# Regrouping rows six slots ahead of their premix, with eight buffers, in a fused attention and expert kernel

## The chip, the cores and the metric

The kernel runs on one core of one Trainium2 chip. The metric is the device time of one execution in microseconds (us). Three executions of the kernel before took 899.65, 904.73 and 894.24 us; their median is 899.65 us.

## The reference, cut to what matters

Three stages follow one another. The first is attention with "talking heads": the heads are mixed before and after the softmax. Here there are 4 batches, 12 heads, 448 positions, and 64 values per head.

```python
scores = scale * np.matmul(q, k.transpose(0, 1, 3, 2))
scores = np.einsum('bhij,hg->bgij', scores, w_pre)
attn = np.exp(scores - np.max(scores, axis=-1, keepdims=True))
attn = attn / (np.sum(attn, axis=-1, keepdims=True) + 1e-09)
attn = np.einsum('bhij,hg->bgij', attn, w_post)
out = np.matmul(attn, v)
```

Its output, as 1792 tokens of 768 values, goes through `h = x @ w_in; (h - tanh(h)) @ w_out` (stage 1) and then through a mixture of 8 experts with 4 slots each. The change lies in the attention and at its border to stage 1.

## The kernel before, in words

**Chunks and slots.** Each batch's 448 query rows are cut into chunks of 120, 120, 120 and 88 rows, 16 chunks in all. A chunk is worked in slots of at most 10 query rows: 12 slots for a chunk of 120, 10 for one of 88, so 184 slots. The chunks start at slots 0, 12, 24, 36, 46, 58, 70, 82, 92, 104, 116, 128, 138, 150, 162 and 174.

**What a chunk and a slot go through.** The scores of a chunk (L275, for two heads a call, six calls) are matmuls whose results ScalarE copies (L295) into a tile `S` with the query row on the partition. There are two `S` tiles, so the scores of chunk m go where those of chunk m-2 were. Head mixing wants the heads of a query row on the partition, so `regroup` (L308) moves the rows of one slot from `S` into a tile `D`, by one DMA on SyncE's queue (SP). There are `DB` of these tiles, used in turn. Two slots make a pair: at every even slot `premix` (L315) multiplies two `D` tiles by the mixing matrix and VectorE takes the maxima (L325); `expo` (L328) is ScalarE's exponential; `guard`, `recip` and `norm` (L337 to L351) make the second mixing matrix divided by the sums; `postmix` (L355) comes four slots later and `gather` (L369) copies its result; `values` (L392) multiplies by v.

**What sets the order.** Every engine works through its instructions in the order in which the program emits them. The main loop (L573) emits, at slot s: the regroup of slot s + `D_AHEAD` (L577), then the loads and stores planned for s (all on SP's queue), then, at an even s, premix, an earlier pair's postmix, expo and guard; at an odd s, recip, norm and gather; then two of the waiting copies of scores, then pieces of a conversion of the weights of stage 1 (loads at L88 and L94, six slots ahead of their use; stores at L120), then at most two waiting jobs (transposes of keys L235 and queries L258, and `values`).

A regroup waits, in SP's queue, for the premix that last read its `D` tile, and for the copies that filled its `S` tile. With `D_AHEAD` = 4 and `DB` = 6 the regroup of slot s + 4 goes to the tile of slot s - 2. The first copy of a chunk's scores into `S` waits until the last regroup of the chunk two before has landed.

**A planner** (L428 to L519) places the other work by slots. The three `head` groups of chunk m (scores of two pairs of heads each) start at the chunk before, at its start minus `D_AHEAD` plus 1 (L451 to L461), two slots after the chunk two before has had its last regroup issued. The keys of a batch are transposed beside them (L462 to L471), their loads at least six slots sooner. A chunk's queries are transposed in two halves in windows (L472 to L477), each in the slot with the least TensorE work planned; the loads of queries have windows of their own, which `D_AHEAD` does not enter. Conversion pieces are spread over the loop (L487). Loads with a window go where SP's plan is emptiest.

**The end.** At slot 184 - `D_AHEAD` (L614) the tiles of keys, queries, `S` and the conversion are given back, and stage 1's first weights and inputs are loaded into their space (L1168 to L1172). Stage 1's first work is emitted after the last slot (L1173).

Of the kernel before, what the change touches and what calls it, by code (L numbers as in the profile page):

```python
# [132 lines left out]
def talking_heads(tc, ident, q, k, v, w_pre, w_post, xd, box, follow):  # L133
# [2 lines left out]
    NC = len(chunks)  # L136
    slots = [(n, kk) for n in range(NC) for kk in range(len(chunks[n][3]))]
    NS = len(slots)
    D_AHEAD = 4
    DB = 6  # L140
    T_LAG = 4
    EB = T_LAG // 2 + 1
    WARM = 10
# [17 lines left out]
    def load_k(b, p):  # L161
        if b:
            t = er.tile([JP, NR, 2, HD], FP32, tag="kn", name="kn", bufs=NP)
            nc.sync.dma_start(out=t, in_=k[b, 2 * p:2 * p + 2].rearrange("e (p r) d -> p r e d", r=NR))
        else:
            t = er.tile([JP, 2, NR, HD], FP32, tag="kn", name="kn", bufs=NP)
            nc.sync.dma_start(out=t, in_=k[b, 2 * p:2 * p + 2].rearrange("e (p r) d -> p e r d", r=NR))
        nat_k[b, p] = t
# [8 lines left out]
    def load_q(n):  # L177
        b, i0, ni, _ = chunks[n]
        t = er.tile([CHUNK, NH, HD], FP32, tag="qn", name="qn")
        nc.sync.dma_start(out=t[:ni], in_=q[b, :, i0:i0 + ni, :].rearrange("h p d -> p h d"))  # L180
        nat_q[n] = t
# [121 lines left out]
    def rows(s):  # L303
        n, kk = slots[s]
        o, m = chunks[n][3][kk]
        return n, o, m

    def regroup(s):  # L308
        n, o, m = rows(s)
        t = ds[s % DB]  # L310
        ni, w = chunks[n][2], len(chunks[n][3])
        nc.sync.dma_start(out=t[4:4 + m * NH], in_=S_t[n][o:ni:w])
        D_t[s] = t
# [114 lines left out]
    start = [sum(len(c[3]) for c in chunks[:n]) for n in range(NC + 1)]  # L428
# [8 lines left out]
    def fetch(lo, hi, cost, f, *a):  # L437
        wanted.append((hi, lo, cost, f, a))

    def calm(kind, lo, hi):  # L440
        return min(range(lo, hi + 1), key=lambda s: (load[kind][s], s))

    def job(s, f, *a, act=0.0, dve=0.0, pe=0.0):
        plan("job", s, f, *a)
        load["pe"][s] += pe
        load["act"][s] += act
        load["dve"][s + 1] += dve

    for m in range(1, NC):
        w = len(chunks[m - 1][3])  # L450
        w0 = start[m - 1] - D_AHEAD  # L451
        for g in range(3):
# [9 lines left out]
    for m in range(1, NC):  # L462
        if chunks[m][1] + CHUNK >= SEQ and m + 1 < NC:
            w = len(chunks[m - 1][3])
            w0 = start[m - 1] - D_AHEAD
            free_at = {}
# [5 lines left out]
    for m in range(2, NC):  # L472
        t0 = start[m - 2]
        if m > 2:
            fetch(max(2, t0 - 12), t0 - 8 if t0 > 12 else max(2, t0 - 7), 0.7, load_q, m)
        for lo, hi, hf in ((max(2, t0 - D_AHEAD + 1), t0 + 3, 0), (t0 + 4, start[m - 1] - D_AHEAD - 1, 1)):
            job(calm("pe", lo, hi), q_half, m, hf, act=0.47, dve=0.53, pe=0.4)  # L477
    for m in range(NC):
        step = len(chunks[m + 1][3]) // 3 if m + 1 < NC - 1 else 2
        for g in range(3 if m + 1 < NC else 0):  # L480
            lo = start[m + 1] + T_LAG + 1 + g * step
# [4 lines left out]
    for i, j in enumerate(pieces):  # L486
        due = 6 + i * (NS - D_AHEAD - 17) // len(pieces)  # L487
        t0 = max(t, due)
# [36 lines left out]
    for p in (1, 2):  # L525
        load_k(0, p)
    ds = [lt.tile([128, SEQ], FP32, tag=f"D{i}", name="D", bufs=1) for i in range(DB)]
    et = [lt.tile([128, SEQ], FP32, tag=f"e{i}", name="e", bufs=1) for i in range(2 * EB)]
# [31 lines left out]
    load_q(2)  # L560
    for s in range(D_AHEAD):
        regroup(s)
# [10 lines left out]
    while s < NS:  # L573
        now[0] = s
        box["both"] = s < NS - D_AHEAD
        if s + D_AHEAD < NS:
# [862 lines left out]
def fused_kernel(  # L1439
# [57 lines left out]
    with tc.manual_schedule():  # L1497
        talking_heads(
            tc, ident, q, k, v, w_pre, w_post, xd, box,
            lambda: moe_and_slots(tc, ident, xd, wi, wo, wo4, wis, (tshift, tlimit, moe2_phi, sel, sela, seld), moe2_w1, moe2_w2, out, box))  # L1500
# [29 lines left out]
```

## Time and profile before

| | before |
|---|---|
| median of three executions | 899.65 us (894.24 to 904.73) |
| profiled execution | 899.93 us |
| span from first to last instruction | 898.2 us |
| mean granted TensorE clock | 0.978 |
| TensorE (PE) busy | 823.1 us, 92% |
| ScalarE (ACT) busy | 573.5 us, 64% |
| VectorE (DVE) busy | 556.1 us, 62% |
| SP's DMA queue, share of 16 engines | 74.4% over the span |

The attention takes the first 444 us or so of the span. All rows are of the one profiled execution, whose own time is 1.7 us above its span. In a row of the timeline a bracket says how long the engine sat idle before it and what ended that wait; the letters q after an engine's name mean its sequencer, which issues DMAs. Where several DMAs share a semaphore the name of the DMA in a bracket can be that of another DMA on the same semaphore.

### The profile page before, as it was taken

Reading aid. Unit: us, or ns where it says so; the run is one execution under the profiler, and the core shown is the slowest. Engines: PE = TensorE matmul, PEld = TensorE weight load, DVE = VectorE, ACT = ScalarE, POOL = GpSimd, SP = SyncE. Lnnn points to the kernel's source line nnn. Section 1 sums busy time; section 2 is a strip of 40 time slices with the busy share of each in tenths; the row PEclk is TensorE's granted clock in tenths of the full one; section 3 lists DMA queues with packets and bytes.
Section 4 is the critical chain, followed back from the end, with each engine's and each line's share of the span. In section 5 each row is a group of like instructions: output and inputs, shape, how many; then the busy total and the mean of one; then the engine's idle time right before and its main releaser. Section 6 shows DMA issues by size and latency. Waiting matters only on the chain.

```text
span 898.2 us, 28617 instructions
## 1 busy us (share of the span) xinstructions
PE 823.1 (92%) x11760; PEld 581.5 (65%) x11760; DVE 556.1 (62%) x1181; ACT 573.5 (64%) x1351; POOL 257.0 (29%) x438
## 2 busy tenths in 40 slices
PE   8878989889987999999999899999999989999995
PEld 6456666666655666666776676767767767864542
DVE  4456857677766777777467886557776767720103
ACT  4766877778867788878656775647555656621013
POOL 6343434444434334434212561000000035500000
PEclk9989999999999999999999999999999999997998
DMA  6988889887989888774869976688745445899997
GB/s 133 227 215 231 220 215 235 238 226 215 226 217 236 233 208 243 238 216 154 261 216 374 346 243 215 258 306 325 284 162 176 158 141 193 284 380 426 416 372 267
DMA packets 145622, 222.95 MB, mean 248 GB/s; under 512 B 60820, under 2 KB 127444, under 8 KB 142036
## 3 DMA queue, kind: packets, MB, share of 16 engines
q1 hardware_dynamic: 142144, 208.26, 74.4%
q10 hardware_dynamic: 3348, 12.87, 3.6%
q8 instruction: 93, 1.52, 0.7%
q14 instruction: 37, 0.30, 0.1%
HBM read 146.39 MB, written 36.18 MB: 203 GB/s over the span
## 4 chain that ended last, share of the span: by engine, by line
PE 57%; ACT 13%; DMA 12%; DVE 12%; issue 4%; POOL 1%; SPq 0%; ACTq 0%; POOLq 0%; DVEq 0%
PE hp L830 21%; DMA D<-S 9%; PE pm L321 5%; ACT e L333 5%; PE vx L403 5%; PE sc L287 4%; PE tm L364 4%; DVE mx L325 3%; PE h L1314 3%; ACT S L295 2%; PE so L1355 2%; PE gt L900 2%; PE tz L1334 2%; ACT aT L378 2%; PE lgp L984 2%
## 5 line engine op out<-in xcount | busy, mean ns | idle before, releaser
L333 ACT ACTIVATE e<-pm,mx 128x448 f32<-128x448 f32 x184 | 115.1, 632 | 81.8 <-DVE mx L325 78.5
L830 PE MATMUL hp<-xa,rg 128*128 128x512 f32 x576 | 153.1, 405 | 0.6 <-ACT xa L813 0.4
L325 DVE TENSOR_REDUCE mx<-pm 128x1 f32<-128x448 f32 x184 | 106.1, 618 | 76.2 <-PE pm L321 76.0
L364 PEld LDWEIGHTS tm<-wk,e 64*56 64x56 f32 x5888 | 108.5, 130 | 57.0 <-issue 30.7
L321 PE MATMUL pm<-D,wpre 64*64 64x448 f32 (+2 forms) x736 | 113.0, 566 | 19.1 <-DMA D<-S 16.8
L364 PE MATMUL tm<-wk,e 64*56 64x60 f32 x5888 | 117.5, 218 | 10.1 <-issue 5.3
L830 PEld LDWEIGHTS hp<-xa,rg 128*128 128x128 f32 x576 | 102.2, 188 | 30.0 <-issue 10.5
L295 ACT ACTIVATE S<-sc 120x448 f32<-120x448 f32 (+1 forms) x186 | 91.4, 552 | 13.8 <-DMA kn<-in_k_dram 5.8
L287 PE MATMUL sc<-khi,qT 64*120 64x448 f32 (+1 forms) x384 | 84.0, 395 | 9.2 <-DVE xs L413 6.5
L787 POOL TENSOR_TENSOR rg<-rg 128x384 fp32r<-128x384 f32 x32 | 32.0, 1012 | 207.0 <-DVE rg L784 195.2
L339 POOL TENSOR_SCALAR rv<-ss 128x2 f32<-128x2 f32 x92 | 24.5, 267 | 229.1 <-ACT e L333 191.0
L350 POOL TENSOR_SCALAR wk<-wpost,rv 128x60 f32<-128x60 f32 x184 | 85.2, 494 | 16.2 <-DVE rv L343 14.5
L403 PE MATMUL vx<-aT,vn 128*64 128x120 f32 (+1 forms) x1536 | 85.3, 263 | 3.7 <-issue 3.2
L403 PEld LDWEIGHTS vx<-aT,vn 128*64 128x64 f32 x1536 | 74.8, 138 | 10.5 <-issue 5.6
L860 DVE SCALAR_TENSOR_TENSOR qd<-qd,sq 128x512 f32<-128x512 f32 (+1 forms) x62 | 38.3, 617 | 64.1 <-ACT mk L856 57.6
L849 ACT ACTIVATE sq<-hp 128x512 f32<-128x512 f32 (+1 forms) x62 | 32.8, 529 | 70.4 <-PE hp L830 70.2
L378 ACT ACTIVATE aT<-tm 128x480 f32<-128x480 f32 x144 | 75.8, 593 | 0.4 <-PE tm L364 0.4
L830 PE MATMUL hp<-xb,rg 128*128 128x512 f32 x288 | 74.7, 404 | 0.0
L287 PEld LDWEIGHTS sc<-khi,qT 64*120 64x120 f32 (+1 forms) x384 | 46.3, 176 | 26.1 <-PE tm L364 7.9
L830 PEld LDWEIGHTS hp<-xb,rg 128*128 128x128 f32 x288 | 52.0, 188 | 16.6 <-issue 6.3
L321 PEld LDWEIGHTS pm<-D,wpre 64*64 64x64 f32 (+2 forms) x736 | 24.8, 132 | 56.8 <-DMA D<-S 22.6
L71 POOL TENSOR_TENSOR fa<-fa,f 128x384 f32<-128x384 f32 x56 | 57.4, 1026 | 7.2 <-DVE rv L343 3.4
(194 smaller groups left out, 1407.9 us busy)
## 6 DMA issues: line engine op xcount, KB each, us to landing
ex<-in_moe_w_dram SPq DMA_DIRECT2D x25, 1536.0 KB
D<-S SPq DMA_DIRECT2D x144, 210.0 KB
rg<-wis SPq DMA_DIRECT2D x32, 768.0 KB
f<-in_moe_w_in_dram SPq DMA_DIRECT2D x32, 384.0 KB
wis<-rg ACTq DMA_DIRECT2D x16, 768.0 KB
rg<-wi SPq DMA_DIRECT2D x26, 384.0 KB
f<-in_moe_w_out_dram SPq DMA_DIRECT2D x24, 384.0 KB
wi<-fa SPq DMA_DIRECT2D x32, 192.0 KB
```

What stands on the lines that cost most here:

```text
L71: eng.tensor_tensor(out=out, in0=bits(a), in1=bits(p), op=ALU.add)
L287: nc.tensor.matmul(xs[e][0][:ni], lhsT=qT[n][s, l, p, :ni], rhs=kt[s], start=(i == 0), stop=(i == 2))
L295: nc.scalar.activation(out=dst, in_=xs[e][0][:ni], func=ACTF.Copy)
L321: nc.tensor.matmul(xs[x][64 * i:64 * i + 64], lhsT=wpre[k0:k1], rhs=d[i][k0:k1], start=True, stop=True)
L325: nc.vector.tensor_reduce(out=mx[:, x:x + 1], in_=xs[x], op=ALU.max, axis=AX.X, negate=True)
L333: nc.scalar.activation(out=es[x], in_=xs[x], func=ACTF.Exp, bias=mx[:, x:x + 1], accum_out=ss[:, x:x + 1])
L350: nc.gpsimd.tensor_scalar(out=wk, in0=wpost, scalar1=rv[:, x:x + 1], scalar2=None, op0=ALU.mult)
L364: nc.tensor.matmul(xs[i][64 * z:64 * z + JH, x, c], lhsT=es[x][h, j:j + JH], rhs=wks[x][h], start=True, stop=True)
L378: nc.scalar.activation(out=out[:, :, c0:c0 + m].rearrange("p a (x i) -> p a x i", x=2), in_=x, func=ACTF.Copy)
L403: nc.tensor.matmul(x[64 * e:64 * e + 64, i, :ni], lhsT=nat_v[b, h // NP][:, h % NP, c, :], rhs=a[:, c, h, :ni], start=(c == 0), stop=(c == ...
L830: nc.tensor.matmul(hp, lhsT=r32(w[:, m, hl, cs]), rhs=r32(x_of(b, c, l)), start=(c == 0 and i == 0), stop=(c == KD - 1 and i == 2))
L860: nc.vector.scalar_tensor_tensor(out=qd, in0=qd, scalar=TG_E, in1=sq, op0=ALU.add, op1=ALU.mult)
```

## The change: what it does

`D_AHEAD` goes from 4 to 6 and `DB` from 6 to 8. Regroups are issued six slots ahead of their slot and into eight tiles, so the regroup of slot s + 6 goes to the tile of slot s - 2. Six regroups instead of four are issued ahead of the loop, and at each slot the loads and stores stand behind regroups that are two slots further on. Everything that is counted from `D_AHEAD` comes two slots sooner: the scores of each chunk (two of the three groups of chunk 1 now stand ahead of the loop, instead of one), the transposes of keys with the latest slots of their loads, the windows of the first halves of the queries, and the slot at which stage 1's first loads are emitted (178 instead of 180). The last slot for the second half of the queries stays where it was, as the +1 makes up for the larger `D_AHEAD`. The conversion's 56 pieces are spread over 161 slots instead of 163.

```diff
-    D_AHEAD = 4
-    DB = 6
+    D_AHEAD = 6
+    DB = 8
...
-        for lo, hi, hf in ((max(2, t0 - D_AHEAD + 1), t0 + 3, 0), (t0 + 4, start[m - 1] - D_AHEAD - 1, 1)):
+        for lo, hi, hf in ((max(2, t0 - D_AHEAD + 1), t0 + 3, 0), (t0 + 4, start[m - 1] - D_AHEAD + 1, 1)):
             job(calm("pe", lo, hi), q_half, m, hf, act=0.47, dve=0.53, pe=0.4)
```

## Rows read from the trace of the kernel before

**Rows 1.** The page: the span in 40 slices, granted clock and DMA share in tenths

```profile
PEclk9989999999999999999999999999999999997998
DMA  6988889887989888774869976688745445899997
```

**Rows 2.** Waits of TensorE, 0 to 445 us: who, for whom, total us, times, longest

```profile
PE pm L321 <- DMA D<-S: 16.8, 18, 2.7
```

**Rows 3.** Timeline at slots 44 and 56: start, length, instruction, [idle before it]

```profile
121.48 2.37 SPq L312 DMA_DIRECT2D D<-S  x2
...
130.15 0.60 PE L321 MATMUL pm<-D,wpre 64*64 64x448 f32 x3 [1.93 <-DMA D<-S]
...
130.37 0.98 ACT L295 ACTIVATE S<-sc 120x448 f32<-120x448 f32 x2 [3.21 <-DMA kn<-in_k_dram]
...
158.37 0.60 PE L321 MATMUL pm<-D,wpre 64*64 64x448 f32 x3 [1.56 <-DMA D<-S]
...
158.43 0.98 ACT L295 ACTIVATE S<-sc 120x448 f32<-120x448 f32 x2 [2.64 <-DMA kn<-in_k_dram]
```

**Rows 4.** Line L295, copies into S: ScalarE's idle time by releaser, us and times

```profile
  DMA kn<-in_k_dram: 5.8, 2
...
  DMA D<-S: 2.0, 2
  DMA f<-in_moe_w_in_dram: 1.5, 1
```

**Rows 5.** Windows: length, busy us (count) of PE PEld DVE ACT POOL, clock, DMA, GB/s

```profile
134.15:163.40 29.25, 26.30 (x573) 18.52 (x571) 19.45 (x47) 22.55 (x63) 12.57 (x24) 0.94 0.91 233
...
351.84:376.76 24.92, 23.03 (x572) 16.16 (x571) 19.22 (x45) 21.71 (x62) 11.43 (x23) 1.00 0.80 237
43.00:50.00 7.00, 4.31 (x74) 2.53 (x72) 3.89 (x10) 4.15 (x11) 2.74 (x6) 0.76 0.91 221
155.00:164.00 9.00, 7.44 (x124) 5.37 (x124) 3.89 (x10) 5.62 (x14) 3.53 (x7) 0.81 0.88 227
```

**Rows 6.** DMA issues in 134.15 to 163.40 us: line, count, KB each

```profile
D<-S SPq DMA_DIRECT2D x13, 210.0 KB
f<-in_moe_w_in_dram SPq DMA_DIRECT2D x2, 384.0 KB
f<-in_moe_w_out_dram SPq DMA_DIRECT2D x2, 384.0 KB
kn<-in_k_dram SPq DMA_DIRECT2D x3, 224.0 KB
wi<-fa SPq DMA_DIRECT2D x2, 192.0 KB
wo<-fa SPq DMA_DIRECT2D x2, 192.0 KB
xd<-xs SPq DMA_DIRECT2D x1, 360.0 KB
qn<-in_q_dram SPq DMA_DIRECT2D x1, 360.0 KB
```

**Rows 7.** Timeline of the start, 12 to 35 us

```profile
12.16 2.52 POOL L540 MEMSET D<- 4x448 f32 x6
...
23.84 0.47 PE L287 MATMUL sc<-khi,qT 64*120 64x448 f32 x2
...
26.06 0.23 POOL L339 TENSOR_SCALAR rv<-ss 128x2 f32<-128x2 f32 x1 [2.82 <-ACT e L333]
...
30.12 0.82 SPq L180 DMA_DIRECT2D qn<-in_q_dram  x1
...
34.69 1.58 PE L321 MATMUL pm<-D,wpre 64*64 64x448 f32 x8
```

**Rows 8.** Timeline at the border to stage 1

```profile
434.70 0.78 SPq L766 DMA_DIRECT2D rg<-wi  x1
...
443.44 0.88 ACT L777 ACTIVATE rg<-rg 128x768 fp32r<-128x768 f32 x1
```

## Prediction

> **What bounds the kernel now.** I read the page's slices first: in the attention (slices 1 to 20) DMA is busy 7 to 9 tenths, and the granted clock is full but for a few slices [rows 1]. TensorE is busy 92% of the span, so what can be won in the attention is its waits. TensorE's list of waits has one large entry: premix waits for a regroup 18 times, 16.8 us in all, at most 2.7 us [rows 2]. Then I read where they lie. The page's slices cannot tell that, but two windows that span the same piece of work can. Chunk 4 (slots 46 to 57, 134.15 to 163.40 us) and chunk 12 (slots 138 to 149) do the same number of matmuls, 573 and 572; one takes 29.25 us with DMA at 0.91, the other 24.92 us with DMA at 0.80 [rows 5]. So a calm pair of slots takes 24.92 / 6 = 4.15 us, and the waits come in bursts in which the DMA engines are full. The 18 waits lie in three: about 25 to 80 us, 118 to 190 us and 240 to 300 us.
>
> The third reading decides the forecast. At slot 44 TensorE's premix is released at 130.15 us, after 1.93 us of waiting, and ScalarE's first copy of the next chunk's scores into S is released at 130.37 us, after 3.21 us [rows 3]. Both wait for one landing: the regroup of slot 45 is the last that reads the old S (it was issued in the group of two that starts at 121.48). The bracket names a key load, but the copy writes S, which only regroups read. The same double release stands at 158.37 and 158.43 us for slot 57 [rows 3]. ScalarE waits in this way at five copies named in the line's list, 5.8 + 2.0 + 1.5 = 9.3 us [rows 4]. So there are two limits on a late DMA: the six D buffers, and the two S buffers. The change deepens only the first.
>
> **The price of one transfer.** In the full stretch from 134.15 to 163.40 us SP issues 13 + 2 + 2 + 3 + 2 + 2 + 1 + 1 = 26 transfers [rows 6], so one costs 29.25 / 26 = 1.125 us of a full DMA system.
>
> **The change part by part.**
>
> *Regroups two slots further ahead, eight buffers.* A regroup still waits for the premix of the pair that starts two slots before the loop's slot, because 6 - 8 = 4 - 6, so SP runs no further ahead of TensorE than it did. What changes is the order in its queue: a premix now needs the loads and stores of six slots before it, not four. In a burst that starts from a calm point, two regroups are already done and two slots' loads are no longer in front. That is about four transfers, 4 x 1.125 = 4.5 us of relief for premix.
>
> *Scores two slots sooner.* The copy into S must happen two slots sooner too, 4.15 us, while the same four transfers are gone from in front of its regroup. 4.5 - 4.15 leaves about nothing on average, so I counted transfers by the planner's rules, worked through for both values, up to the last regroup of a chunk. From loop slot 34 to the regroup of slot 45: before 7 regroups and 11 others (three stores, one query load, one key load, three conversion loads, two of v, one output); after 5 and 6. Seven fewer are 7.9 us against 4.15: the 3.21 us wait there goes. To slot 69, the end of that burst, it is 69 against 64: five fewer, 5.6 - 4.15 = 1.5 us gained. To slot 115, from loop slot 88: 50 against 46, 4.5 - 4.15 = 0.35 us gained. In the first burst nothing is calm before, all starts with S: to slot 23 it is 24 regroups and 19 others against 24 and 16, 3.4 - 4.15 = 0.8 us lost. Sum: 1.0 us gained. What is late next is thus ScalarE's copy, one pair before the premix that used to wait. Behind it ScalarE holds the exponentials of the next pair, and for those TensorE and VectorE wait. The bounds: if ScalarE's waits cost TensorE nothing, 16.8 us gained [rows 2]; if no regroup is done ahead (a burst that starts full), two transfers less against a pair sooner, 4.15 - 2.25 = 1.9 us lost in each of three bursts, 5.7 us. I take the count, being worked for this order.
>
> *The clock.* Around 47 us the granted clock is 0.76 over 7 us, around 159 us 0.81 over 9 us [rows 5]: 7 x 0.24 = 1.7 and 9 x 0.19 = 1.7 us of full-speed work lost. Each holds a stretch at the lower level, 1.2 GHz, behind waits for regroups; there are four of that kind (47, 60, 77 and 159 us), 6.8 us. Some will stay, as the copies' waits idle TensorE too. I take half, 3.4 us, and keep 0 and 6.8.
>
> *The start.* Two more memsets of 2.52 / 6 = 0.42 us are hidden by 2.82 us in which GpSimd waits for the first exponential [rows 7]. The second group of chunk 1's scores moves ahead of the first premix; in the loop it started at 23.84 us [rows 7], so it delays the first pair by what the first pair gives back: 0, at worst the 1.5 us of its twelve matmul pairs. Chunk 3's first queries are transposed at slot 8 instead of 10, their load stays at slot 5. It was issued at 30.12 us; with the 8.7 us that a regroup took in a burst (121.48 to 130.15 [rows 3]) it lands at 39, while slot 8's premix starts at 34.69 [rows 7]. A wait of up to 3 us there is covered by the longer one for slot 23 that follows; without that cover it would be 3 us more. The later query loads come 3 to 8 slots ahead instead of 5 to 10, mostly in calm stretches: 0, up to 1 us each for three of them.
>
> *Stage 1's loads.* They are issued from 434.70 us, and ScalarE reads the first weights at 443.44 us with no idle time marked before it [rows 8]. That is 8.7 us of lead already, so two slots more bring 0. All regroups are issued a slot before these loads in both versions, so SP is not held up by them. Keys, conversions (two slots fewer for 56 pieces) and other orders of the planner: 0.
>
> **Sum**: 1.0 + 3.4 = 4.4 us gained. The profiled execution took 899.93 us, 0.28 above the median, so the forecast is 895.5 us.
>
> **Rivals.**
>
> *The buffers were the limit.* If ScalarE catches up after its wait, premix's 16.8 us go and half of the clock's: 899.9 - 16.8 - 3.4 = 879.7 us. For it speaks that TensorE's list names no other large wait [rows 2]. Against it: ScalarE is busy 21.71 of 24.92 us in a calm chunk, 87% [rows 5], so it catches up by only half a microsecond a pair, and its copies were released by the same landings [rows 3]. The Trainium skill has the rule behind this rival: its page "Perfetto Trace Analysis", section "Identifying Performance Opportunities", says that a gap that repeats on the engine that should be full can mean too little buffer space for the next tile. By that rule alone more D tiles bring the 879.7. The trace agrees only in part, since chunk 12 shows no such gaps with the same six buffers.
>
> *The wait at S grows: slower.* The scores come a pair sooner, but the queue in front of their regroup shrinks by only two transfers wherever a burst starts full. Place: the first copy into S of the chunks that start in the three bursts. Price: 1.9 us each at two chunk borders a burst, 11.4 us, with no clock won back: 911 us. It decides from the point where fewer than 4.15 / 1.125 = 3.7 transfers are gone from in front. The first burst is below that (3), the others above (5 and 4).
>
> *Nothing moves.* If the queue is so full that regroups land when they did, whatever their place, the time stays at 899.9 us. For it: DMA at 0.91 in bursts [rows 5]; against it: calm stretches at 0.80 lie between.
>
> **How the numbers follow.** Forecast 0.47, buffers 0.26, S grows 0.13, nothing moves 0.14. The forecast's own range is 889 to 902: at best 1.0 + 6.8 for the clock + 3.2 for a wait like slot 45's, at worst the count is one transfer short in each burst, 1.0 - 3 x 1.125, with no clock won. The whole range cuts the buffers' case in half and leaves out the upper part of the slower one, 0.13 + 0.07 together: 881 to 907. One per cent, which is about what a measurement of this kernel can tell from no change, is 9.0 us: faster is below 890.7, slower above 908.6. Faster: the buffers' case and a little of the forecast, 0.29. Slower: most of the S case, 0.11. Same: 0.60.
>
> **What the profile after would show.** TensorE's entry "premix waits for a regroup" should fall from 16.8 to under 5 us, while ScalarE's idle time before copies into S rises from 9.3 to 15 us or more, at slots 19, 53, 65, 99 and 113. The window of chunk 4 should be between 25 and 28 us long. Stage 1's first weights are read after the last gather as before. I am wrong if the waits at S don't rise and the attention shortens by more than 10 us (then the D buffers were the limit), or if premix still waits 10 us (then the queue was).

## The result: 0.8% slower, and the profile after

The kernel after takes 907.11 us in the median (902.60 to 911.49, 20 runs), the kernel before 901.07 (894.24 to 912.87, 20 runs beside them). The ratio is 1.0081 with a 95% interval of 1.0062 to 1.0100: 6 us slower, where 4.4 us faster was forecast, and 0.1 us above the upper end of the range (881 to 907). The profiled execution of after took 903.14 us (span 901.4, mean granted clock 0.971), 4 us under its median.

Where a run's span and mean granted clock are on record, it can be split: span times (1 - clock) is the time that TensorE's half speed took if TensorE was busy throughout, span times clock is the rest. The 20 runs of before beside after have no clock on record, so its row is taken from the runs beside the experiments. The split below, and every ratio, leaves out single runs over 1.5% above the fastest of their kernel (13 of 109 of before, none of after); with them before reads 19.6 and 880.0.

| | runs | lost to the clock, us | the rest, us |
|---|---|---|---|
| before (beside the experiments) | 96 | 19.1 (standard error 0.4) | 879.5 (0.3) |
| after | 20 | 29.4 (0.8) | 876.3 (0.5) |

**In after 10.3 us more stand under half speed, and the rest is 3.2 us shorter.** The first number is a bound, since a half-speed stretch in which TensorE waits costs nothing, and the runs show by how much it overstates. Among runs of one kernel, one more us in the first column goes with only 0.5 to 0.6 us more of span (slope 0.47 to 0.62 within the rounds of before, 0.55 in after; standard errors 0.08 to 0.11), so the rest falls by the other 0.4 to 0.5. By these slopes 10.3 us are an estimated 5 to 6 us of time, about the whole difference, and the 3.2 us are no more than the split alone would give: they do not show that work was won.

The page's slices of after, clock and DMA [rows 1]: in the attention the clock's tenths dip in slices 2 and 4, where they dipped in slice 3 before.

```profile
PEclk9898999999999999999999999999999999998998
DMA  6798899886998878884759976588754435889998
```

TensorE's waits in the first 445 us of after (who, for whom: us in total, times, longest) [rows 2]:

```profile
PE sc L287 <- DVE xs L413: 13.5, 18, 2.4
PE tm L364 <- issue: 8.0, 9, 1.8
PE kx L240 <- ACT S L295: 7.7, 6, 3.2
PE sc L287 <- DVE qT L270: 6.9, 5, 1.7
PE tm L364 <- ACT aT L378: 3.4, 9, 0.8
PE vx L403 <- ACT S L295: 3.1, 5, 0.8
```

The same entries in before:

```profile
PE sc L287 <- DVE xs L413: 6.5, 13, 0.6
PE tm L364 <- issue: 5.3, 5, 1.4
PE kx L240 <- ACT S L295: 4.3, 5, 0.9
PE sc L287 <- DVE qT L270: 0.8, 1, 0.8
```

The premix's wait for D, 16.8 us before, is not in after's list at all. In its place stand waits that end at VectorE's reading of a PSUM bank (xs, qT) and at ScalarE's copies into S. "Issue" means that the profile shows nothing that the engine waited for; more on these below. ScalarE's idle time before its copies into S in after [rows 4]:

```profile
  PE sc L287: 12.4, 13
  DMA wi<-fa: 4.7, 1
  DMA D<-S: 2.2, 1
  DMA f<-in_moe_w_in_dram: 1.6, 1
```

Chunk 4, the burst of the forecast, is 26.19 us long at full clock, though 604 matmuls instead of 573 now stand in it [rows 5], and two windows elsewhere in after lie wholly at half speed (length, busy us of PE, PEld, DVE, ACT, POOL, clock, DMA, GB/s):

```profile
136.34:162.53 26.19, 24.15 (x604) 17.86 (x603) 18.96 (x49) 21.24 (x59) 11.15 (x23) 1.00 0.92 241
29.48:36.31 6.83, 5.88 (x84) 3.97 (x84) 1.78 (x4) 2.08 (x6) 1.06 (x3) 0.50 0.86 249
73.86:80.68 6.82, 6.11 (x56) 4.52 (x60) 1.23 (x3) 3.65 (x10) 2.05 (x4) 0.50 0.88 234
```

Four places in after's timeline show the new waits (start, length, instruction, [idle before it]). **The start** [rows 7]:

```profile
25.50 0.63 ACT L333 ACTIVATE e<-pm,mx 128x448 f32<-128x448 f32 x1 [0.80 <-DVE mx L325]
...
26.32 1.54 PE L321 MATMUL pm<-D,wpre 64*64 64x448 f32 x8 [1.54 <-issue]
...
28.25 0.46 PE L287 MATMUL sc<-khi,qT 64*120 64x448 f32 x1
...
29.84 0.53 DVE L270 TENSOR_TENSOR qT<-qx,qT 128x360 fp32r<-128x360 f32 x1
...
30.43 0.73 PE L287 MATMUL sc<-khi,qT 64*120 64x448 f32 x1 [1.73 <-DVE qT L270]
...
32.96 1.77 PE L321 MATMUL pm<-D,wpre 64*64 64x448 f32 x8
```

The second premix waits 1.54 us; its row names no releaser, but the first exponential ends at 26.13, just before it. The score group that filled this gap before has moved ahead of the loop. Then a query's transpose (slot 2) stands right ahead of a score group (slot 3). A group takes all four small banks of PSUM, and the transpose's bank is given back only by VectorE's subtraction, which the code issues in the next slot: 1.73 us more. The half-speed stretch from 29.48 us begins within this wait.

**A query's second half in the slot before a score group**, slots 40, 86 and 132; here slot 41:

```profile
124.36 0.51 DVE L270 TENSOR_TENSOR qT<-qx,qT 128x360 fp32r<-128x360 f32 x1
...
124.93 0.63 PE L287 MATMUL sc<-khi,qT 64*120 64x448 f32 x1 [1.47 <-DVE qT L270]
```

**The one buffer of xs**: SP issues the store of a chunk's output at 173.53, and VectorE's copy of the next chunk's first values, which holds a bank, waits for its landing; the score group behind waits for the bank:

```profile
173.53 0.60 SPq L390 DMA_DIRECT2D xd<-xs  x1
...
181.71 0.57 DVE L413 COPY xs<-vx 128x240 f32<-128x240 f32 x1 [2.05 <-DMA xd<-xs]
...
182.42 0.40 PE L287 MATMUL sc<-khi,qT 64*88 64x448 f32 x1 [2.35 <-DVE xs L413]
```

**ScalarE before S at slot 19**, and the keys' transposes that wait for its bank:

```profile
71.89 0.97 ACT L295 ACTIVATE S<-sc 88x448 f32<-88x448 f32 x2 [4.74 <-DMA wi<-fa]
...
72.48 0.61 PE L240 MATMUL kx<-ident,kn 112*128 112x112 f32 x4 [3.23 <-ACT S L295]
```

At the border stage 1's loads are issued 2.7 us later than before, and the first weights are read 4.6 us later, as the attention is that much behind there [rows 8]:

```profile
437.36 0.67 SPq L766 DMA_DIRECT2D rg<-wi  x1
...
448.05 0.87 ACT L777 ACTIVATE rg<-rg 128x768 fp32r<-128x768 f32 x1
```

### The profile page after: what moved, and what is told of

The parts are those of the page before. It is cut to its first block, busy times and chain, and to the rows that moved or that the text cites. A ratio compares the mean times of both kernels' runs of the same rounds, so it can differ in the third digit from the quotient of the medians.

```text
span 901.4 us, 28638 instructions
## 1 busy us (share of the span) xinstructions
PE 815.5 (90%) x11760; PEld 580.5 (64%) x11760; DVE 557.3 (62%) x1181; ACT 573.9 (64%) x1351; POOL 259.3 (29%) x440
## 2 busy tenths in 40 slices
DMA packets 145622, 222.95 MB, mean 247 GB/s; under 512 B 60820, under 2 KB 127444, under 8 KB 142036
## 4 chain that ended last, share of the span: by engine, by line
PE 58%; DVE 13%; DMA 11%; ACT 10%; issue 6%; SPq 1%; POOL 1%; ACTq 0%; POOLq 0%
PE hp L830 20%; PE sc L287 6%; PE pm L321 6%; PE vx L403 5%; DMA D<-S 4%; ACT e L333 4%; DVE mx L325 4%; PE tm L364 3%; PE h L1314 3%; DMA xd<-xs 3%; PE gt L900 2%; PE so L1355 2%; PE tz L1334 2%; PE lgp L984 2%; DMA rg<-wi 2%
## 5 line engine op out<-in xcount | busy, mean ns | idle before, releaser
L364 PEld LDWEIGHTS tm<-wk,e 64*56 64x56 f32 x5888 | 106.1, 132 | 73.2 <-issue 43.6
L364 PE MATMUL tm<-wk,e 64*56 64x60 f32 x5888 | 113.3, 220 | 17.9 <-issue 10.5
L287 PE MATMUL sc<-khi,qT 64*120 64x448 f32 (+1 forms) x384 | 89.6, 402 | 23.8 <-DVE xs L413 13.5
L321 PE MATMUL pm<-D,wpre 64*64 64x448 f32 (+1 forms) x736 | 100.3, 589 | 5.6 <-issue 2.9
L295 ACT ACTIVATE S<-sc 120x448 f32<-120x448 f32 (+1 forms) x186 | 91.0, 550 | 21.0 <-PE sc L287 12.4
L350 POOL TENSOR_SCALAR wk<-wpost,rv 128x60 f32<-128x60 f32 x184 | 87.4, 504 | 20.1 <-DVE rv L343 18.1
L287 PEld LDWEIGHTS sc<-khi,qT 64*120 64x120 f32 (+1 forms) x384 | 51.3, 180 | 41.2 <-issue 12.8
L287 PE MATMUL sc<-klo,qT 64*120 64x448 f32 (+1 forms) x192 | 52.1, 395 | 0.0
```

Source lines behind the costliest of these rows:

```text
L287: nc.tensor.matmul(xs[e][0][:ni], lhsT=qT[n][s, l, p, :ni], rhs=kt[s], start=(i == 0), stop=(i == 2))
L295: nc.scalar.activation(out=dst, in_=xs[e][0][:ni], func=ACTF.Copy)
L321: nc.tensor.matmul(xs[x][64 * i:64 * i + 64], lhsT=wpre[k0:k1], rhs=d[i][k0:k1], start=True, stop=True)
L350: nc.gpsimd.tensor_scalar(out=wk, in0=wpost, scalar1=rv[:, x:x + 1], scalar2=None, op0=ALU.mult)
L364: nc.tensor.matmul(xs[i][64 * z:64 * z + JH, x, c], lhsT=es[x][h, j:j + JH], rhs=wks[x][h], start=True, stop=True)
```

## The experiments

Each ratio is to the kernel before in the same round, with its 95% interval; "lost" and "rest" are the split from above (the expectations quote it as it stood when each was written). The medians are over all runs of a row; e9 to e12 come from a round in which before took 905.3 in the median of 11 runs, in the other rounds it took 901.1 to 901.7.

| run | median us | ratio | lost | rest |
|---|---|---|---|---|
| after | 907.1 | 1.0081 (1.0062 to 1.0100) | 29.4 | 876.3 |
| e1 xs in two buffers | 908.0 | 1.0078 (1.0039 to 1.0117) | 26.3 | 878.6 |
| e2 queries away from scores | 907.0 | 1.0068 (1.0031 to 1.0104) | 26.9 | 877.2 |
| e3 start | 905.4 | 1.0055 (1.0019 to 1.0092) | 24.2 | 878.7 |
| e4 = e1 + e2 + e3 | 903.7 | 1.0036 (1.0003 to 1.0070) | 22.5 | 879.1 |
| e17 = e4 + later S in three chunks | 900.4 | 1.0006 (0.9973 to 1.0039) | 21.7 | 877.4 |
| e5 regroups alone, five ahead | 902.3 | 0.9988 (0.9953 to 1.0024) | 21.0 | 876.5 |
| e16 = e5 + e1 | 899.9 | 1.0008 (0.9976 to 1.0039) | 21.3 | 877.5 |
| e6 scores one slot sooner, regroups six | 908.4 | 1.0068 (1.0032 to 1.0104) | 26.5 | 878.9 |
| e7 after, groups closer together | 905.0 | 1.0044 (1.0018 to 1.0070) | 23.8 | 879.5 |
| e8 before, groups closer together | 918.4 | 1.0191 (1.0150 to 1.0232) | 26.3 | 889.7 |
| e11 e4, groups in odd slots | 910.4 | 1.0136 (1.0074 to 1.0197) | 25.3 | 883.9 |
| e12 e4, conversions and close as before | 914.9 | 1.0158 (1.0089 to 1.0228) | 26.7 | 884.5 |
| e9 after, filled waits | 973.6 | 1.0857 (1.0783 to 1.0932) | 63.1 | 910.0 |
| e10 before, filled waits | 924.1 | 1.0250 (1.0177 to 1.0323) | 34.0 | 885.4 |
| e13 before without loads | 872.1 | 0.9687 (0.9654 to 0.9721) | 13.6 | 856.9 |
| e14 after without loads | 887.2 | 0.9853 (0.9823 to 0.9884) | 18.4 | 866.7 |
| e15 e4 without loads | 879.3 | 0.9758 (0.9721 to 0.9795) | 14.0 | 862.8 |
| e18 e5 without loads | 874.3 | 0.9713 (0.9680 to 0.9746) | 14.7 | 857.3 |

**e1 to e4: three of the new waits taken away, one by one and together.**

```diff
# e1
- xs_t[n] = lt.tile([128, NP, CHUNK], FP32, tag="xs", name="xs", bufs=1)
+ xs_t[n] = lt.tile([128, NP, CHUNK], FP32, tag="xs", name="xs", bufs=2)
# e2
- (t0 + 4, start[m - 1] - D_AHEAD + 1, 1)
+ (min(t0 + 4, start[m - 1] - D_AHEAD - 1), start[m - 1] - D_AHEAD - 1, 1)
# e3
- s0 = max(s0, -1)
+ s0 = max(s0, -1) if m > 1 else (-1, 1, 4)[g]
```

> The kernel after (median 907.1), with two buffers for xs instead of one; nothing else changes. Theory (the earlier scores and queries push other work together, and one of the places is the copy of a chunk's values, which now waits for the store of the chunk before): the three waits of TensorE behind that copy (2.35, 1.73 and 2.15 us in the trace after) go, 6.2 us, and the time falls to 899 to 903, ratio to before 0.998 to 1.002. Rival 1 (ScalarE's wait before it writes S is the cost): the waits move to that place and the time stays 905 to 908. Rival 2 (regroups six slots ahead cost by themselves, in the DMA queues): the DMA waits stay, 905 to 908.

> The kernel after, with the second half of a query's transposes put at least one slot away from the score group that follows (window ends two slots sooner). Theory: the three waits of TensorE for the query's residual at slots 41, 87 and 133 (1.47, 1.22, 1.68 us, 4.4 in sum) go, and with them part of the clock that they cost: 901 to 904. Rivals 1 and 2: the same waits go, but what is limited elsewhere stays, 905 to 908.

> The kernel after, with chunk 1's three score groups at slots -1, 1 and 4 instead of -1, -1 and 3. Theory: the premix of slot 0 comes 1.8 us sooner, and the wait of 1.73 us at 30.4 us for the query's residual goes; the premix of slot 12 comes back by 3 to 4.4 us and the half clock from 29.5 to 36.3 us goes, if the rest keeps it: 902 to 904. If a later limit (S or the DMA queues) takes it back: 905 to 908, with the premix of slot 36 as late as in the trace after.

> The kernel after, with the three edits together (two buffers for xs, the queries a slot away from the scores, chunk 1's score groups at -1, 1 and 4). Theory: the three sums 6.2, 4.4 and 3.5 add up but for what is taken back, 14 us at most from 907: 893 to 899, ratio to before 0.991 to 0.998. Rivals 1 and 2: what is bound by S or by the queues stays, 902 to 907.

Alone, none can be told from after by its time, and all four came out slower than the theory's time (e1 899 to 903, e2 901 to 904, e3 902 to 904, e4 893 to 899): where a wait went, others took up its length. What e3 changes shows in one window, from 22 to 40 us. In the kernel before:

```profile
22.00:40.00 18.00, 16.46 (x275) 9.59 (x276) 8.43 (x20) 14.64 (x39) 6.24 (x18) 1.00 0.87 231
```

In the kernel after:

```profile
22.00:40.00 18.00, 13.86 (x190) 7.98 (x189) 6.00 (x13) 10.95 (x30) 5.56 (x11) 0.81 0.72 219
```

In e3:

```profile
22.00:40.00 18.00, 15.22 (x276) 9.47 (x276) 8.46 (x20) 14.24 (x38) 6.41 (x16) 1.00 0.80 235
```

That is 275 matmuls before, 190 after and 276 with e3, at a clock of 1.00, 0.81 and 1.00. Over its runs e3 loses 24.2 us (standard error 0.7) to the clock against 29.4. All three together give 3.4 us of the 6, and 6.9 of the 10.3 us of clock; the rest grows by 2.8, as the slopes above would have it.

**e5 and e6: the parts of the change.** e5 moves the regroups alone; e6 is after with all but the regroups at five slots instead of six.

```diff
# e5, on the kernel before (scores, keys, queries, conversions, close: D_AHEAD = 4)
+ R_AHEAD = 5
- DB = 6
+ DB = 7
- if s + D_AHEAD < NS:
-     regroup(s + D_AHEAD)
+ if s + R_AHEAD < NS:
+     regroup(s + R_AHEAD)
# e6, on the kernel after, with e2: D_AHEAD = 5, R_AHEAD = 6
```

> The kernel before, with the regroups alone moved: five slots ahead of the premix with seven buffers, scores, keys, queries, conversions and the close as before (four slots). So the first copy into S comes three slots instead of two behind the last regroup that reads that buffer, and D one slot sooner. Theory A (ScalarE's wait to write S takes the time that the premix no longer waits: what limits a chunk is the loop from the last regroup's landing over the copies to the next regroups): both waits shrink, the premix's 16.8 us for D to under 8 and ScalarE's before S from 13.8 to under 8, and the time falls to 889 to 896. Theory B (the earlier scores, keys and queries lose the time at PSUM's small banks, and D's waits were worth nothing because something else follows): 898 to 903. Theory C (the transfers themselves are the limit: about 1.1 us each, whenever they are issued): 898 to 903, with the D waits gone or moved.

> The kernel after, with scores, keys, queries, conversions and the close only one slot sooner than before (five), the queries a slot away from the scores, and the regroups six ahead with eight buffers as after. Theory A (S): ScalarE's wait before S falls from 21 us to under 12, and the time to 893 to 899. Theory B (moving the scores costs): half of what was lost comes back, 901 to 905. Theory C (transfers): 900 to 907, the waits in other places.

The regroups alone are level with before: no harm, and not theory A's gain. But one slot more takes only 3.8 us off the premix's waits for D (16.8 to 13.0); six slots and eight buffers alone were not run. e6 is as slow as after, though the scores move only one slot; they now fall into the premix's even slots, so it does not stand between the two cleanly.

**e7, e8 and e11: ScalarE's wait before S, by putting the score groups closer together.**

```diff
# e7 (after) and e8 (before): slots 3, 6, 9 of the window instead of 1, 5, 9
- s0 = w0 + HEAD_LAG + g * w // 3
+ s0 = w0 + HEAD_LAG + g * w // 3 + (2 - g if m > 1 else 0)
...   (the keys' transposes, which stand behind the groups, move with them)
# e11, on e4: slots 3, 5, 9 (3, 5, 7 in chunks of ten)
```

> The kernel after, with the three score groups of a chunk closer together, the last where it was and the first two slots later (chunk 1 excepted): ScalarE reaches a free S two slots later. Theory A: ScalarE's idle time before S falls from 21 us to under 8, TensorE's wait for S with it, and the time falls to 893 to 900. Theory B: the score groups two and three slots apart meet more jobs at the banks, 905 to 912. Theory C: 903 to 908.

> The kernel before, with the same edit to the score groups. Theory A: ScalarE's idle time before S falls from 13.8 us to under 5, but the regroups of a chunk are issued no sooner, so the premix's waits for D stay near 16.8 us: 896 to 901. Theory B: more conflicts at the banks, 902 to 907. Theory C: 899 to 903.

> The kernel of the three edits together (two buffers for xs, queries a slot away from the scores, chunk 1's groups at -1, 1 and 4), with the score groups of the other chunks in slots 3, 5 and 9 behind the window's start (3, 5 and 7 in chunks of ten) instead of 1, 5 and 9 (1, 4 and 7): always odd slots, away from the premix, and ScalarE reaches S two slots later. Clock theory: ScalarE's wait of 5.7 us before S at slot 19 goes, and with it the half-speed stretch of 6.8 us at slot 21; lost to the clock from 22.5 to 17 to 20, the time 896 to 901. Rival (the groups' spacing makes as many conflicts at the banks): 902 to 908.

In e7 no copy into S waits for a transfer any more; the line's idle time is one entry:

```profile
  PE sc L287: 10.5, 14
```

and the time is 905.0, some 2 us under after. That alone doesn't refute theory A, that S takes back what D gave: the same edit costs the kernel before 17 us (e8, slower by 1.9%), so in e7 a gain at S could be hidden. e14 below decides it. e11 has a ratio of 1.0136, but against the median of its round it is 5 us behind, not clearly more than e4. That closer groups meet more jobs at the banks is the likely reason for e8, and not shown.

**e9 and e10: waits filled with matmuls that nobody reads.**

```diff
+ def fill(n):
+     for i in range(n):
+         nc.tensor.matmul(tws[0][:, 480:512], lhsT=ident, rhs=ident[:, :32], start=True, stop=True)
...
# e9 (after): 20 behind slot 0's premix, 20 before the groups of 41, 65, 87, 99, 111, 133,
#             30 and 15 before the jobs of 20 and 21;  e10 (before): 20 before premix 12, 14, 16, 44, 56, 96
```

> The kernel after, with matmuls that nobody reads (128x128 by 32 columns, into spare columns of a PSUM bank) in front of the TensorE waits that its trace shows: 20 behind the premix of slot 0, 20 before the score groups of slots 41, 65, 87, 99, 111 and 133, 30 and 15 before the keys' transposes of slots 20 and 21; 185 in all, about 1.2 us for 20. Nothing is moved. New theory (the clock): over the runs so far, span times (1 - granted clock) is 29.4 us for the kernel after and 19.6 for the kernel before, and span times clock 876.3 against 880: the change wins 3.7 us of work and loses 9.8 to half speed, because its waits are fewer and longer and each is followed by a stretch at half speed. Then the loss falls from 29.4 to about 18 and the time to 895 to 900. Rival (the waits themselves are the loss, the clock only goes along): the loss stays near 29 and the extra matmuls add up to some us, 906 to 912.

> The kernel before, with 20 such matmuls in front of the premix of slots 12, 14, 16, 44, 56 and 96, where its trace shows TensorE waiting 1.6 to 2.7 us for D; 120 in all. Clock theory: four of the five half-speed stretches of the attention in that trace stand behind such waits or the like; up to 4 x 1.7 us come back: lost to the clock from 19.6 to 14 to 17, time 895 to 899. Rival: 900 to 905.

Both failed as tests. The filling took 61.0 us, not 11, and the clock fell under it. In e9's trace the group of the filling matmuls (busy us, mean ns) is:

```profile
L540 PE MATMUL tm<-ident 128*128 128x32 f32 x370 | 61.0, 336 | 11.2 <-ACT aT L378 6.4 <-ACT aT L382 4.8
```

A window of e9 that is nearly all filling has PE busy for 19.97 of 21 us, and a clock of 0.59:

```profile
76.00:97.00 21.00, 19.97 (x185) 18.41 (x186) 2.03 (x5) 6.05 (x15) 2.05 (x4) 0.59 0.54 133
```

They neither show nor refute that the pauses cost the clock.

**e12: conversions and the pool's close back at four slots from the end.**

```diff
# on e4: NS - D_AHEAD becomes NS - 4 in due, box["both"] and the close
```

> The kernel of the three edits together, with the weights' conversions, the use of both pairs of small banks and the close of the attention's pool (so stage 1's first loads) as before, four slots from the end instead of six. If the earlier close or the conversions cost: 900 to 902. If they don't (theory): 902 to 906, as with the three edits (903.7).

Slower than e4, against both expectations: by 1.2% by the two ratios, by some 7 us against the medians of their rounds. So these three taken together are no cost of the change, and putting them back moves the time by as much as the whole change. Which of them does it, and by which order, I did not find. A few us of other experiments' gains can likewise come from orders that an edit moved by the way.

**e13 to e15: 51 loads of 384 KB taken away**, 20 MB (222.95 to 202.89 MB over the span) or about a fifth of what the attention moves (some 220 GB/s for 420 us). From the sixth conversion on, no weights are loaded; the conversions run on tiles that are there.

```diff
  def load(self, j):
+     if len(self.raw) == self.bufs and not self.done:
+         self.raw.append(self.raw.pop(0))
+         self.t[j] = [self.raw[-1]]
+         return
...   (and lines that keep the first five tiles at hand, up to the end of the attention)
```

> The kernel before, with the loads of the converted weights left out from the sixth piece on (51 of 56; each conversion works on one of the five tiles that were loaded, its stores stay, and what follows is of the same size, but the weights are wrong). Question: what is left of the difference between the two kernels when the DMA queues are not full? Here: the premix's waits for D fall from 16.8 us to under 5, the time to 882 to 892.

> The kernel after, with the same loads left out. Theory (the pauses at the start, at the queries and at xs, that three edits took away, cost 7 of the 10 us of half speed): ScalarE's DMA waits before S fall from 8.5 to under 2, but these pauses stay, so this is 3 to 8 us slower than the kernel before without the loads. Rival (the full queues turn the earlier scores into waits before S, and these are the loss): no slower than the kernel before without the loads.

> The kernel of the three edits together, with the same loads left out. Theory: with those pauses and the queues both out of the way it is as fast as the kernel before without the loads, or up to 4 us faster, and its loss to the clock as small. Rival: as slow as the kernel after without the loads.

With the queues eased before takes 872.1 (10 us less than expected) and after 887.2. So full queues are not the cause: with fewer loads after is 15.1 us behind instead of 6. As the regroups alone cost nothing (e5, and e18 below), the cost lies in what else moved: scores, keys, queries, conversions and the close. It isn't ScalarE's waiting for transfers before S either, theory A, which is 3.8 us in e14's trace and 4.2 in e13's. e4's three edits give back 7.9 of the 15.1; e15 came out neither as fast as e13 nor as slow as e14, and what holds the other 7 stays open. TensorE's waits without the loads, before:

```profile
PE pm L328 <- DMA D<-S: 7.4, 8, 1.8
...
PE sc L294 <- DVE xs L420: 4.5, 10, 0.6
PE kx L247 <- ACT S L302: 4.3, 5, 0.9
...
PE sc L294 <- DVE qT L277: 0.8, 1, 0.8
```

and after:

```profile
PE sc L294 <- DVE xs L420: 8.5, 19, 0.7
PE kx L247 <- ACT S L302: 7.9, 7, 2.3
PE sc L294 <- DVE qT L277: 6.0, 5, 1.5
...
PE vx L410 <- ACT S L302: 2.5, 3, 0.8
...
PE pm L328 <- DMA D<-S: 0.3, 1, 0.3
```

D's waits fall by 7.1 us; xs, kx and qT alone grow by 4.0 + 3.6 + 5.2 = 12.8. No xs wait is longer than 0.7 us now (2.4 with the loads), but there are 19 instead of 10. The clock takes 4.8 us more than in e13 (18.4 against 13.6).

**e16: the better half with e1.**

```diff
# e5 and e1 together
```

> The regroups alone five slots ahead with seven buffers (as in the run of that, 902.3 against 901.6), and two buffers for xs: does the better half of the change, with the store's wait taken away, beat both kernels? If the waits behind the copy of the values (4.9 us in that trace) are worth what they show: 895 to 899. If other waits take them over, as with the kernel after: 899 to 903.

Level with before: no version that beats both.

**e17: the last of the four places**, S at slot 19, on top of e4.

```diff
+ if m in (3, 7, 11) and g == 0:
+     s0 += 2
- t = w0 + HEAD_LAG + p // 2 * w // 3 + 1 + p % 2
+ t = w0 + (6, 7, 7, 10, 10, 11)[p]
```

> The kernel of the three edits together (903.7), with one more: for chunks 3, 7 and 11 the first score group two slots later (slot 21 instead of 19 for chunk 3), and the keys' transposes of the next batch, which must stand behind it, in slots 24, 25, 25, 28, 28 and 29 instead of 20, 21, 24, 25, 28 and 29. Aimed at ScalarE's wait before S at slot 19 (5.7 us in that trace, TensorE's keys wait for it, half speed for 6.8 us from 71.5), the one pause that the kernels with the scores two slots sooner share. Theory: wait and stretch go, 3.4 us of clock and 1 to 3 of wait: 897 to 901, level with the kernel before or just under it. If the full queues only move the wait to D or another chunk: 902 to 906.

900.4 us, level with before, and clear of after: 0.9973 to 1.0039 against 1.0062 to 1.0100. The window from 68 to 82 us in e4:

```profile
68.00:82.00 14.00, 8.92 (x134) 6.79 (x124) 5.42 (x12) 7.25 (x19) 2.18 (x5) 0.76 0.92 222
```

The same window in e17, 247 matmuls at a clock of 1.00 against 134 at 0.76:

```profile
68.00:82.00 14.00, 12.35 (x247) 8.73 (x247) 9.85 (x25) 12.42 (x31) 5.54 (x11) 1.00 0.89 224
```

**e18: the regroups alone without the loads.**

```diff
# e5 with the edit of e13
```

> The regroups alone five slots ahead with seven buffers, scores and all else as before, and the loads of the converted weights left out from the sixth piece on (51 of 56, so the weights are wrong). With those loads the regroups alone were level with the kernel before (902.3 to 901.6), without them the kernel before takes 872.1. If the earlier regroups are a gain that the full queues hide: 866 to 870, with the premix's 7.4 us for D under 3. If not: 871 to 874.

No gain with the queues eased either: 874.3 against 872.1. The premix still waits 5.4 us for D there, not under 3.

## Why the prediction was wrong

*Regroups further ahead: right for the wait.* The premix's wait went from 16.8 us to nothing; "under 5" was said. Chunk 4 came out at 26.19 us, between the 25 and 28 forecast. Whether it brought the 1.0 us counted can't be read from the times.

*Scores two slots sooner: half right.* I priced this step through S alone. At slot 19 the count said 0.8 us lost; ScalarE waits 4.74 us there. Over the attention the idle time put down to transfers did not rise as I said: 4.7 + 2.2 + 1.6 = 8.5 us against 9.3 [rows 4], while the part put down to scores that came late grew from 4.3 to 12.4.

*The steps that failed* are "Keys, conversions [...] and other orders of the planner: 0", the start at 0, and the clock's 3.4 us. The term for the query loads held: no wait for one is in after's list. I did not ask what the moved transposes, values and score groups stand next to. All share four PSUM banks; a bank filled in one slot is read out by VectorE in the next, and a score group needs all four. Before, no query, key or value job stood in the slot right before a score group; after, four do (slots 2, 40, 86, 132, the "+ 1" of the diff's last line among them). The values kept their windows while the scores moved, so 33 instead of 28 of the 45 stand two slots ahead of a group, by the planner's rules. After is 6 us slower for what moved beside the regroups, and 15.1 us with eased queues (e13, e14); four local edits bring it level (e17, with the full queues). The Trainium skill, page "Perfetto Trace Analysis", section "Matmuls", says that independent groups of matmuls should go round different PSUM banks, so that one's readout overlaps the next one's work. The traces agree: where the readout is one slot late, the group waits 1.47 us (slot 41).

*The clock: wrong sign.* I took half of 6.8 us as won back, 0 at worst; 10.3 us more stood under half speed, by the slopes some 5 to 6 us of time. In the attention of after's trace the clock falls nine times, in before's five. The 6.8 was misread too: the stretch at 77 us stands behind a post-mix's wait of 1.41 us that names no releaser, not behind a wait for a regroup, so three stretches were of that kind. Pauses and half speed go together: where a pause was removed (e3, e17), the profiled window returns to 1.00. I had looked for half speed only behind waits that would go, not behind waits that would come. Neither of my two signs of being wrong came, as both asked about D and S alone.

*The rivals.* "The buffers were the limit" fell with after and e17, where the premix waits 0 and 3.9 us for D and no time is won; a single slot more for D, too, is worth nothing that these runs can tell, with or without full queues (e5, e16, e18). The rule of the Trainium skill behind it ("Perfetto Trace Analysis", "Identifying Performance Opportunities") held in its first half only: the repeating gap went with more buffers, and the time did not get shorter. "The wait at S grows" had the right side and one right place, slot 19, worth some 3 us (e17 against e4); e14 shows that it is not the main cause.

*What took up D's 16.8 us.* In e17, where the new waits are repaired, no gain is left. Its trace, of one of its slower executions (904.81 us), has one large new entry, post-mixes that wait for nothing the profile shows:

```profile
PE tm L364 <- issue: 17.9, 10, 4.7
...
PE pm L321 <- DMA D<-S: 3.9, 3, 3.5
```

D's waits fell by 12.9 us from before, and this entry rose by 12.6. The longest lies inside one post-mix of 64 like matmuls, behind the 53rd:

```profile
335.47 0.90 PE L364 MATMUL tm<-wk,e 64*56 64x60 f32 x53
...
341.10 0.65 PE L364 MATMUL tm<-wk,e 64*56 64x60 f32 x11 [4.73 <-issue]
```

TensorE has 13 "issue" waits in the first 445 us of e17, 12 in after and 8 in before; 12, 11 and 8 of them end 1.3 to 1.8 us after a packet of the trace's DMA queue "instruction" has landed (here at 339.47). So TensorE probably stood there for its own next instructions, held up in the full queues: with the loads left out the entry is 4.0 to 5.6 us (e13, e14, e15, e18), and in e12, slow without a reason found, 18.5. That an earlier D only moves the wait to there is not shown: it is one trace a kernel, and no run tests it.

## What to carry to other kernels

When a change moves an operation in a fixed order, list for each moved one what now stands in front of and behind it and which banks they share; ask it of those that did not move as well. Weigh pauses by the granted clock too, over many runs, and check the split by its slope among runs of one kernel: here 10.3 us more at half speed went with 6 us of time, which no list of waits shows. Look also at waits that name no releaser. And to learn what a reordering costs by itself, take away the load that hides it: the eased kernels told 15 us where the full ones told 6.

## What the runs showed of the hardware

In e9 the granted clock fell while TensorE was at work without a pause. The filling matmuls, 128x128 by 32 columns, took 0.33 us each (61.0 / 185); they ran on from 73.31 to 81.81 us, the clock fell to half at 78.30 and stayed there until 95.37, and over 76 to 97 us TensorE was busy for 19.97 of 21 us at a mean clock of 0.59. Half speed also came behind short pauses: behind 1.47 us at slot 41 in after (half from 125.06 us for 3.4 us), and from 46.55 us behind one of 0.74 us. And 51 loads fewer were worth 29.5 us to the kernel before (901.6 to 872.1), though its list of waits named only 16.8 us of the premix's waiting for transfers.
